# Strided attention in blocks of one residue group instead of blocks of three, and another order for batch 0

## The chip, the cores and the metric

The kernel runs on one core of one Trainium2 chip. A core has a matrix engine (TensorE, PE in the profile, with its weight loads listed as PEld), VectorE (DVE), ScalarE (ACT), GpSimd (POOL) and SyncE (SP). Here POOL and SP also issue the transfers: POOL those that change the type from fp32 to bf16 on the way, SP the plain ones and the transposing ones. The metric is the device time of one execution in microseconds.

## What is computed

Eight batches of eight heads, 576 positions, head size 64. Heads 0 to 3 attend to the last 32 positions ("local"), heads 4 to 7 to all earlier positions with the same residue modulo 32 ("strided"). The outputs of the heads stand side by side as x, with 4608 rows of 512, and go through two matrix products with a squared ReLU between them.

```python
mask_local = (rel >= 0) & (rel < stride)                      # stride = 32
mask_strided = (rel >= 0) & (pos[None, :] % stride == pos[:, None] % stride)
scores = np.where(masks[None, :, :, :], scale * q @ k.T, -1e9)
attn = softmax(scores)
x = (attn @ v).transpose(0, 2, 1, 3).reshape(B * S, H * D)    # 4608 x 512
out = np.maximum(x @ w_in, 0) ** 2 @ w_out                    # 512 -> 2048 -> 512
```

## The kernel before

**Units.** A unit `u` is one pair of heads of one batch, `u = 4 * b + p`; pairs 0 and 1 are local, 2 and 3 strided. A local pair is cut in six blocks of 96 queries, each with 128 keys. A strided pair is cut by residues: positions with equal residue modulo 8 (or 16) form a small dense problem with a mask.

**Strided blocks.** In batches 0 and 1 (`u` up to 7) a strided head has eight blocks, one for each `j = position mod 8`, of 72 positions each. From batch 2 on the kernel before uses the residue modulo 16: 36 positions for each of 16 residues, three residues together in one block of 108 and two in the last of 72, so three blocks for each half of a head (`KB`, `BLK`, lines 39 to 41). `mask_blk` is the mask for them. In the output step the sums come from a column of ones that stands beside V in the tile `vs`.

**Steps of a unit.** `step_T` transposes Q and K of a local pair on PE, `step_TS` those of the strided pairs of batches 0 and 1. `step_S` forms the scores (lines 342 and 350), ACT takes the exponential (360), VectorE multiplies by the mask (367). `step_D` multiplies by V (436) in two parts of six blocks, each into one PSUM bank, and VectorE divides by the sum (446, 447). `step_E` brings the result into `xt`, which holds x transposed: by PE and a copy (483, 485), by a transposing transfer of `x_l` (469), or, for the strided pairs of the last two batches, through DRAM (`x_d`, 463 and 465). `step_N` and `step_O` take the place of D and E for the strided pairs of batches 0 and 1.

**PSUM.** There are eight banks in three rings: `ph` (2), `py` (1) and `pt` (5). Scores take four `pt` banks, each part of D one, each E on PE one.

**Order.** Everything is written out by hand. `first_steps` lists batch 0. Then a list `groups` holds the two products chunk by chunk (512 rows of x each): `mm1` is the first product with ReLU on ACT (511) and the square on VectorE (514), `mm2` the second (545). Before each group the loop takes as many attention steps as `due` says, which spreads each batch's steps over the groups before the first chunk that needs them. Loads hang on group numbers (`second`, `plan`). All engines run their own instructions in that program order.

**Transfers.** POOL issues, in this order for batches 2, 3 and 4: the rows of Q and K of local pairs (135), the copies `q_d`, `k_d` of strided Q and K into DRAM in bf16 (172), then, behind a gate that waits for the transposed `kT_s` (line 626), V of the local pairs (`vl`, 235 and 236) and V of the strided pairs (`vs`, 637). SP transposes `q_d` and `k_d` into `qT_s` and `kT_s` (178), stores the output (553), and for batch 4 first waits in `hold_sync` (630) until the last strided V has landed. For batches 5 to 7 SP loads Q, K (119), V (218 and 251), and POOL casts them (145, 225, 226, 257, 258). In batch 0 POOL loads V of both local pairs with one pair of transfers (235, 236), before w_in (692).

Of the kernel before, what the change touches and what calls it, by code (L numbers as in the profile page):

```python
# [14 lines left out]
def kernel(  # L15
# [23 lines left out]
    PS16 = NA * STRIDE // 16  # L39
    KB = 3 * PS16  # L40
    BLK = ((0, KB), (KB, KB), (2 * KB, S // 2 - 2 * KB))
    V0 = 4
# [36 lines left out]
    mask_blk = singles.tile([KB, 1, S // 2], BF16)  # L79
    vl_all = singles.tile([128, NV, 2, NL, VP], BF16, name="vl")  # L80
    vls = [vl_all[:, i] for i in range(NV)]
    vss = [singles.tile([KB, 2, 3, 2 * D + 8], BF16, name=f"vs{i}") for i in range(NV)]
# [84 lines left out]
    def cast_str_dram(b):  # L167
        for name, src in (("q", q), ("k", k)):
            t = dram.tile([2 * S, 2 * D], BF16, name=f"{name}_d")
            tv = t.rearrange("(h j p) c -> h p j c", h=4, j=8)  # L170
            for h in range(4):
                nc.gpsimd.dma_start(out=tv[h], in_=src[b, 4 + h].rearrange("(p j r) d -> p j (r d)", j=8, r=2))  # L172
            big[b, name] = t

    def transpose_str(b):
        for name in "qk":
            o = strT.tile([128, NJ // 2, 4 * SP_], BF16, name=f"{name}T_s").rearrange("c a n -> c (a n)")
            nc.sync.dma_start_transpose(out=o, in_=big.pop((b, name)))
            came[b] = o[0:1, 0:1]
            for i in range(2):  # L180
                st.setdefault(4 * b + 2 + i, {})[name + "T"] = o[:, S * i:S * (i + 1)]
# [49 lines left out]
    def load_v_local_sw(b):  # L231
        i = (2 * b) % NV
        t = vl_all[:, i:i + 2].rearrange("p u h t d -> p (u h t) d")[:, :, 0:D]
        src = v[b, 0:4].rearrange("h (t p) d -> p (h t) d", p=QL)
        nc.gpsimd.dma_start(out=t[32:128], in_=src)  # L235
        nc.gpsimd.dma_start(out=t[0:32, 1:4 * NL], in_=src[64:96, 0:4 * NL - 1])
        for u in range(2):
            st.setdefault(4 * b + u, {})["v"] = vls[i + u]

    def v_str_pieces(u):  # L240
        b, p = units[u]
        for h in range(2):
            vv = v[b, 2 * p + h].rearrange("(p x r) d -> p x (r d)", x=8, r=2)
            for j in range(3):
                n = 3 if j < 2 else 2
                yield slice(PS16 * j, PS16 * (j + 1)), h, slice(0, n), vv[:, j:j + 3 * n - 2:3, :]

    def load_v_str(u, eng):
        t = v_st.tile([KB, 2, 3, 2 * D], FP32, name="v_st")
        for rows, h, blks, src in v_str_pieces(u):  # L250
            eng.dma_start(out=t[rows, h, blks], in_=src)
        st.setdefault(u, {})["vf"] = t

    def cast_v_str(u):
        s = st[u]
        t = vss[v_slot(u)]
        nc.gpsimd.tensor_copy(t[:, :, 0:2, V0:V0 + 2 * D], s["vf"][:, :, 0:2])
        nc.gpsimd.tensor_copy(t[0:BLK[2][1], :, 2, V0:V0 + 2 * D], s["vf"][0:BLK[2][1], :, 2])
# [56 lines left out]
    def step_S(u, at_once=False):  # L315
# [3 lines left out]
        blocks = not local and u > 7  # L319
        w, n = (QL, NL) if local else (SP_, NJ)  # L320
        kn = 128 if local else KB if blocks else SP_
        hn = 3 if blocks else n // 2
        e = es[u % 4]
        s["e"] = e
        pss = [[None, None], [None, None]]
        for half in range(2):
# [7 lines left out]
            for i in range(hn):  # L334
                t = half * hn + i
                klo = w * t
                for row in range(2):
                    rows = slice(64 * row, 64 * row + 64)
                    if blocks:
                        lo, m = BLK[i]  # L340
                        cols = slice(S // 2 * half + lo, S // 2 * half + lo + m)
                        nc.tensor.matmul(pss[row][half][0:m, lo:lo + m], kT[rows, cols], qT[rows, cols],  # L342
                                         start=True, stop=True)
                        continue
# [7 lines left out]

        for row in range(2):
            for half in range(2):
                unread[id(pss[row][half])] = u

        def expo(row, half):
# [526 lines left out]
```

## Time and profile before

| what | value |
|---|---|
| median of 3 runs | 325.71 us (325.20 to 325.84) |
| profiled execution, its run's time | 325.71 us |
| its span on the core | 324.0 us |
| mean granted TensorE clock | 0.984 |
| PE busy | 303.7 us, 94% |
| VectorE, ScalarE, GpSimd busy | 148.8, 167.5, 112.9 us |
| transferred | 40.76 MB in 113918 packets |

The span is what the profiler saw on the core; the run's time has 1.7 us more around it. Times of a timeline or chain are microseconds from the start of the span. In a list of waits the numbers are the total, how often, and the longest. A group line has the busy time in us, the mean of one instruction in ns, and behind the second bar the time that the engine stood idle just before these instructions, with what ended it. In the rows of tenths each figure is a fortieth of the span, about 8.1 us.

### The profile page before, as it was taken

What the parts mean: (1) busy time and instruction counts of PE and PEld (TensorE: products, weight loads), DVE (VectorE), ACT (ScalarE), POOL (GpSimd) and SP (SyncE); (2) the same over time, 40 slices, a digit from 0 to 9 for tenths busy, and PEclk for the clock granted to TensorE, in tenths of its full rate; (3) what the DMA queues carried; (4) which work ended last, traced back from release to release, by engine and by line L of the source; (5) the groups of instructions that cost most, each with busy time, mean ns of one, the idle gap of its engine ahead of it and who ended that gap; (6) DMA issues with size and microseconds to landing.
All of it is one profiled execution on the core that took longest, in us unless ns stands there. A gap on an engine that the chain in (4) does not pass through costs nothing.

```text
span 324.0 us, 6032 instructions
## 1 busy us (share of the span) xinstructions
PE 303.7 (94%) x2256; PEld 149.6 (46%) x2256; DVE 148.8 (46%) x389; ACT 167.5 (52%) x346; POOL 112.9 (35%) x170
## 2 busy tenths in 40 slices
PE   7999999979699966999899999999999999999995
PEld 3555454545355532444344444444444444444444
DVE  4458645557456760455555666652532222222200
ACT  4768548856548751455455556554344444344411
POOL 8653421891769963591307721500000000000000
PEclk9999999999979996999999999999999999999999
DMA  8999999979999999889975999534131011001021
GB/s 160 174 202 202 191 193 148 171 92 130 175 136 142 86 120 194 189 109 207 201 164 125 202 213 178 128 85 120 46 75 51 33 55 45 32 32 34 32 97 65
DMA packets 113918, 40.76 MB, mean 126 GB/s; under 512 B 96546, under 2 KB 108898, under 8 KB 113890
## 3 DMA queue, kind: packets, MB, share of 16 engines
q0 software_dynamic: 49120, 15.02, 42.5%
q1 hardware_dynamic: 64770, 25.38, 36.0%
q8 instruction: 17, 0.28, 0.4%
q14 instruction: 11, 0.09, 0.1%
HBM read 37.64 MB, written 13.57 MB: 158 GB/s over the span
## 4 chain that ended last, share of the span: by engine, by line
PE 57%; DMA 22%; POOL 12%; issue 5%; SPq 2%; ACT 1%; DVE 1%; POOLq 0%; DVEq 0%
PE py L545 23%; PE ph L505 23%; DMA vl<-in_v_dram 7%; PE ph L545 5%; POOL vs L637 4%; DMA xt<-x_l 3%; DMA kT_s<-k_d 3%; DMA w_in_b<-in_moe_w_in_dram 3%; DMA k_st<-in_k_dram 2%; POOL q_d L172 2%; PE pt L436 2%; POOL k_d L172 1%; DMA x_d<-x_s 1%; POOL vl L235 1%; PE ph L527 1%
## 5 line engine op out<-in xcount | busy, mean ns | idle before, releaser
L505 PE MATMUL ph<-xt,w_in_b 128*128 128x512 bf16 x552 | 141.1, 381 | 2.5 <-DMA xt<-x_l 1.8
L511 ACT ACTIVATE r<-ph 128x512 bf16<-128x512 f32 x138 | 82.3, 597 | 97.8 <-PE ph L505 96.6
L514 DVE TENSOR_TENSOR g_sb<-r 128x512 bf16<-128x512 bf16 x144 | 62.3, 435 | 124.3 <-ACT r L511 123.7
L545 PE MATMUL py<-w_out_b,g_sb 128*128 128x512 bf16 x400 | 104.5, 384 | 0.0
L505 PEld LDWEIGHTS <-w_in_b 128*128 128x128 bf16 x576 | 53.2, 98 | 60.9 <-issue 4.5
L545 PEld LDWEIGHTS <-g_sb 128*128 128x128 bf16 x560 | 51.4, 99 | 58.0 <-issue 4.5
L360 ACT ACTIVATE e<-pt 128x288 bf16<-128x288 f32 (+2 forms) x128 | 45.8, 410 | 15.8 <-PE pt L350 8.1
L545 PE MATMUL ph<-w_out_b,g_sb 128*128 128x512 bf16 x144 | 36.0, 387 | 2.1 <-ACT r L511 2.1
L436 PEld LDWEIGHTS <-e 128*128 128x128 bf16 (+1 forms) x336 | 17.7, 99 | 17.3 <-issue 6.4
L637 POOL DMA_DIRECT2D vs<-in_v_dram x36 | 22.6, 635 | 4.1 <-DMA vl<-in_v_dram 1.6
L549 ACT COPY y<-py 128x512 f32<-128x512 f32 x25 | 14.6, 585 | 7.0 <-PE py L545 6.7
L172 POOL DMA_DIRECT2D k_d<-in_k_dram x24 | 15.7, 658 | 4.6 <-DMA w_out_b<-in_moe_w_out_dram 1.8
L172 POOL DMA_DIRECT2D q_d<-in_q_dram x24 | 15.8, 664 | 2.7 <-DMA w_out_b<-in_moe_w_out_dram 2.2
L447 DVE TENSOR_TENSOR x_l<-pt,rinv 96x384 bf16<-96x384 f32 x28 | 15.5, 553 | 1.0
L446 DVE RECIPROCAL rinv<-pt 96x6 f32<-96x6 f32 (+1 forms) x52 | 9.8, 189 | 12.1 <-PE pt L436 12.0
L225 POOL CAST vl<-vl_st 128x768 bf16<-128x768 f32 x6 | 5.4, 893 | 27.7 <-DMA vl_st<-in_v_dram 15.1
L436 PE MATMUL pt<-vl,e 128*128 128x65 bf16 x168 | 10.5, 199 | 4.1 <-DMA vl<-in_v_dram 4.1
L367 DVE TENSOR_TENSOR e<-e,mask_full 128x576 bf16<-128x576 bf16 x28 | 13.2, 478 | 1.4 <-ACT e L360 1.2
L447 DVE TENSOR_TENSOR x_s<-pt,rinv 108x384 bf16<-108x384 f32 x24 | 13.4, 558 | 0.8
L549 ACT COPY y<-ph 128x512 f32<-128x512 f32 x9 | 5.2, 583 | 13.4 <-PE ph L545 13.4
L342 PE MATMUL pt<-qT_s,kT_s 64*108 64x108 bf16 x144 | 6.3, 220 | 5.6 <-DMA kT_s<-k_d 5.6
L367 DVE TENSOR_TENSOR e<-e,mask_blk 108x576 bf16<-108x576 bf16 x24 | 11.1, 481 | 0.7 <-ACT e L360 0.7
(120 smaller groups left out, 213.1 us busy)
## 6 DMA issues: line engine op xcount, KB each, us to landing
out_dram<-y SPq DMA_DIRECT2D x35, 256.0 KB
w_out_b<-in_moe_w_out_dram POOLq DMA_DIRECT2D x4, 512.0 KB, 15.2
q_d<-in_q_dram POOLq DMA_DIRECT2D x24, 72.0 KB, 5.0
k_d<-in_k_dram POOLq DMA_DIRECT2D x24, 72.0 KB, 5.4
q_st<-in_q_dram SPq DMA_DIRECT2D x12, 144.0 KB
k_st<-in_k_dram SPq DMA_DIRECT2D x12, 144.0 KB
vl_st<-in_v_dram SPq DMA_DIRECT2D x12, 144.0 KB
vl<-in_v_dram POOLq DMA_DIRECT2D x5, 288.0 KB, 6.1
```

The costliest lines, as they stand in the source:

```text
L172: nc.gpsimd.dma_start(out=tv[h], in_=src[b, 4 + h].rearrange("(p j r) d -> p j (r d)", j=8, r=2))
L360: nc.scalar.activation(e[0:kn, lo:lo + S // 2], pss[row][half][0:kn, 0:S // 2], AF.Exp, scale=scale)
L367: nc.vector.tensor_tensor(x, x, m, op=ALU.mult)
L436: nc.tensor.matmul(po[:, n, :], e[0:kn, pos:pos + 128], rhs, start=True, stop=True)
L446: nc.vector.reciprocal(rinv[0:w], po[0:w, :, dc:dc + 1])
L447: nc.vector.tensor_tensor(x, po[0:w, :, x0:x0 + D], rinv[0:w].to_broadcast([w, 6, D]), op=ALU.mult)
L505: nc.tensor.matmul(ph, w_in_b[:, kk, 128 * ff:128 * (ff + 1)], xt[kk][:, 512 * c:512 * (c + 1)], start=(kk == order[0]), stop=(kk == order ...
L511: nc.scalar.activation(r, ph, AF.Relu)
L514: later(1, lambda: nc.vector.tensor_tensor(g[:, ff, :], r, r, op=ALU.mult))
L545: nc.tensor.matmul(py, g[:, ff, 128 * j:128 * (j + 1)], w_out_b[:, ff, :], start=(ff == 0), stop=(ff == 15))
L549: nc.scalar.copy(y, py)
L637: nc.gpsimd.dma_start(out=t[rows, h, blks, V0:V0 + 2 * D], in_=src)
```

## The change

Strided pairs of batches 2 to 7 have eight blocks of 72 per head, as batches 0 and 1 have. `mask_blk`, `KB`, `BLK` and the two-residue layouts go.

- The copies `q_d` and `k_d` become one transfer each for the four heads, 16 rows of 9216 elements, in place of four transfers of 36x8x128. The transposes read 288 rows of 512 in place of 1152 rows of 128.
- V of a strided pair is loaded by one transfer for a head (72x8x64 into `vs`) in place of three; on SP (batches 5 to 7) by one of 72x2x512 for a pair in place of six. `x_d` is written by one transfer in place of six.
- `step_S` forms 16 products of 72 for 12 of 108 or 72; `step_D` has 16 blocks in three parts (6, 6, 4) for 12 in two; `step_E` on PE has eight transposes for six.
- Batch 0: V of each local pair is loaded by its own two transfers; `step_S` of unit 3 takes its exponentials half by half with part 1 of D of unit 0 between the halves; the copies of `x` of units 0 and 1 go to VectorE; pair 1 comes ahead of pair 2 in `first_order`; the late constants are written ahead of the loads of batch 1.

```diff
 def cast_str_dram(b):
     for name, src in (("q", q), ("k", k)):
-        t = dram.tile([2 * S, 2 * D], BF16, name=f"{name}_d")
-        tv = t.rearrange("(h j p) c -> h p j c", h=4, j=8)
-        for h in range(4):
-            nc.gpsimd.dma_start(out=tv[h], in_=src[b, 4 + h].rearrange("(p j r) d -> p j (r d)", j=8, r=2))
+        t = dram.tile([4 * SP_, NJ * D], BF16, name=f"{name}_d")
+        nc.gpsimd.dma_start(
+            out=t.rearrange("(x y) c -> x (y c)", x=16),
+            in_=src[b, H // 2:H].rearrange("h (x y) d -> (h x) (y d)", x=4))
...
-def load_v_local_sw(b):
-    i = (2 * b) % NV
+def load_v_local_sw(b, u0=0, nu=2):
+    i = (2 * b + u0) % NV
...
 def load_v_str(u, eng):
-    t = v_st.tile([KB, 2, 3, 2 * D], FP32, name="v_st")
-    for rows, h, blks, src in v_str_pieces(u):
-        eng.dma_start(out=t[rows, h, blks], in_=src)
+    b, p = units[u]
+    t = v_st.tile([SP_, 2, NJ * D], FP32, name="v_st")
+    eng.dma_start(out=t, in_=v[b, 2 * p:2 * p + 2].rearrange("h (p j) d -> p h (j d)", j=NJ))
...
 def step_S(u, at_once=False, between=None):
...
-                if blocks:
-                    lo, m = BLK[i]
-                    cols = slice(S // 2 * half + lo, S // 2 * half + lo + m)
-                    nc.tensor.matmul(pss[row][half][0:m, lo:lo + m], kT[rows, cols], qT[rows, cols], ...)
-                    continue
...
+        if between:
+            for row in range(2):
+                expo(row, half)
+            between(half)
...
 def step_D(u, part):
+    if is_local(u):
+        w, kn, n0, n1, tot = QL, 128, 6 * part, 6 * part + 6, 2 * NL
+    else:
+        w, kn, tot = SP_, SP_, NBS
+        n0, n1 = ((0, 6), (6, 12), (12, 16))[part]
...
 def step_E(u):
-        for j in range(3):
-            for r in range(2):
-                nc.sync.dma_start(out=xv[:, 2 * j + r:2 * j + r + 6 * m - 5:6, :], in_=x[PS16 * j:PS16 * (j + 1), r, 0:m])
+        nc.sync.dma_start(out=xd.rearrange("(p j) c -> p (j c)", j=NJ), in_=x.rearrange("p n d -> p (n d)"))
...
-    copy = nc.scalar.copy if u < 12 else nc.vector.tensor_copy
+    copy = nc.scalar.copy if 1 < u < 12 else nc.vector.tensor_copy
...
-first_order = (0, 2, 1, 3)
+first_order = (0, 1, 2, 3)
...
-  (ts("k", 0, v_), 0), (ts("k", 1, s_), 1), (S_(2), 0), (D_(0, 0), 0), (D_(0, 1), 0), (S_(3), 0),
-  (D_(1, 0), 0), (n(2), 1), (E_(0), 0), (n(3), 0), (D_(1, 1), 0),
-  (o(2), 0), (lambda: part((a,)), 0), (E_(1), 0), (o(3), 0), (lambda: part((b,)), 0),
-  (lambda: part((c,)), 0), (lambda: part((d,)), 0)]
+  (ts("k", 0, v_), 0), (ts("k", 1, s_), 1), (S_(2), 0),
+  (D_(0, 0), 0), (lambda: step_S(3, between=lambda half: None if half else step_D(0, 1)), 0), (n(2), 1),
+  (D_(1, 0), 0), (E_(0), 1), (D_(1, 1), 0), (n(3), 0), (lambda: part((a,)), 0), (E_(1), 0),
+  (o(2), 0), (lambda: part((b,)), 0), (lambda: part((c,)), 0), (o(3), 0), (lambda: part((d,)), 0)]
...
 def load_v_str_direct(b):
     for u in (4 * b + 2, 4 * b + 3):
         t = vss[v_slot(u)]
-        for rows, h, blks, src in v_str_pieces(u):
-            nc.gpsimd.dma_start(out=t[rows, h, blks, V0:V0 + 2 * D], in_=src)
+        h = 2 * units[u][1]
+        for i in range(2):
+            nc.gpsimd.dma_start(out=t[:, NJ * i:NJ * (i + 1), 0:D],
+                                in_=v[b, h + i].rearrange("(p j) d -> p j d", j=NJ))
...
-load_v_local_sw(0)
+load_v_local_sw(0, 0, 1)
+load_v_local_sw(0, 1, 1)
...
-loads_1()
 late_constants()
+loads_1()
```

## The prediction

> **What bounds the kernel now.** I read the page's head first, then the waits of PE, then PE's timeline around each wait, then the timelines of POOL, SP and ACT back from there. The first fence is the page: PE is busy 94% of the span, and its clock falls to 7 and 6 tenths in two slices near 90 and 124 us.
>
> ```profile
> PE 303.7 (94%) x2256; PEld 149.6 (46%) x2256; DVE 148.8 (46%) x389; ACT 167.5 (52%) x346; POOL 112.9 (35%) x170
> PE   7999999979699966999899999999999999999995
> PEclk9999999999979996999999999999999999999999
> ```
>
> So the end is set by PE, and only two things can move it: matmuls that PE has more or fewer of, and the holes. From 18 us on the holes sum to 14.0 us. The next fence, the waits of PE (total, times, longest), names them.
>
> ```profile
> PE pt L342 <- DMA kT_s<-k_d: 5.6, 1, 5.6
> PE pt L436 <- DMA vl<-in_v_dram: 4.1, 3, 3.0
> PE ph L545 <- ACT r L511: 2.1, 1, 2.1
> PE ph L505 <- DMA xt<-x_l: 1.8, 2, 1.6
> ```
>
> In PE's timeline three lie between 70 and 125 us: 2.13 us before 73.41, 3.04 + 0.70 us before 90.08, and 5.55 us before 124.39. The two longer ones cost twice: a group of four 128x512 matmuls that else takes 0.865 us took 1.69 us at 90.80 and 1.68 to 1.71 us from 125.09 to 130.72, under a granted clock of 0.50. Counted against the same instructions at full rate, 90.08 to 92.84 lost 1.3 us, and 124.39 to 130.72 lost 3.1 us (6.33 us for work of 3.19). Stalls and clock in this stretch: 2.13 + 3.74 + 5.55 + 1.3 + 3.1 = 15.8 us.
>
> The third fence follows them back. Columns: start, duration, engine, line, operation, and in brackets the idle time before.
>
> ```profile
> 56.88 0.37 POOL L626 COPY vl<-kT_s 1x1 bf16<-1x1 bf16 x1 [6.31 <-DMA kT_s<-k_d]
> 59.48 3.78 POOL L637 DMA_DIRECT2D vs<-in_v_dram  x6
> 63.89 3.73 POOL L637 DMA_DIRECT2D vs<-in_v_dram  x6 [0.63 <-DMA vl<-in_v_dram]
> 68.97 2.65 POOL L172 DMA_DIRECT2D q_d<-in_q_dram  x4
> 71.61 1.95 POOL L172 DMA_DIRECT2D k_d<-in_k_dram  x3
> 72.04 0.83 ACT L145 COPY q_l<-q_st 96x768 bf16<-96x768 bf16 x1 [2.55 <-DMA q_st<-in_q_dram]
> 77.80 1.22 SPq L178 DMA_TRANSPOSE kT_s<-k_d  x1
> 82.37 0.18 POOL L626 COPY vl<-kT_s 1x1 bf16<-1x1 bf16 x1 [7.96 <-DMA kT_s<-k_d]
> 90.08 0.43 PE L436 MATMUL pt<-vl,e 128*128 128x65 bf16 x5 [0.70 <-DMA vl<-in_v_dram]
> ...
> 114.69 0.30 SPq L630 DMA_DIRECT2D hold<-vs  x1
> 116.84 2.06 SPq L178 DMA_TRANSPOSE kT_s<-k_d  x1
> 124.39 0.76 PE L342 MATMUL pt<-qT_s,kT_s 64*108 64x108 bf16 x12 [5.55 <-DMA kT_s<-k_d]
> ```
>
> To be seen: all three holes hang on POOL's queue of DMA issues. After the gate at 56.88 POOL spends 8.1 us on twelve pieces of V (batch 2), issues batch 3's q/k rows at 67.6, and needs until 74.4 for eight copies q_d/k_d (batch 3). ACT's cast waits for the late rows until 72.04; that is PE's first hole. The transposes on SP wait for the copies, kT_s starts at 77.80 and lands at 82.35; only then does the gate let V of batch 3 go (82.9), which lands at 90.08: the second hole. The same string, one batch on, puts the last V piece of batch 4 so late that the hold on SP passes at 114.69, kT_s starts at 116.84 and PE waits until 124.39. A second rule shows at 89.3 to 93.7: successive V pieces wait for vl, vl, q_st and k_st, the transfers eight issues earlier. So POOL has at most eight transfers out, and many small ones use them up.
>
> The prices are in the groups (busy us, mean ns of one):
>
> ```profile
> L637 POOL DMA_DIRECT2D vs<-in_v_dram x36 | 22.6, 635 | 4.1 <-DMA vl<-in_v_dram 1.6
> L172 POOL DMA_DIRECT2D q_d<-in_q_dram x24 | 15.8, 664 | 2.7 <-DMA w_out_b<-in_moe_w_out_dram 2.2
> L172 POOL DMA_DIRECT2D k_d<-in_k_dram x24 | 15.7, 658 | 4.6 <-DMA w_out_b<-in_moe_w_out_dram 1.8
> L235 POOL DMA_DIRECT2D vl<-in_v_dram x5 | 6.0, 1195 | 1.1 <-POOL vl L626 0.7 <-DMA w_in_b<-in_moe_w_in_dram 0.5
> ```
>
> **The change, part by part.**
>
> *POOL, batches 2 to 4.* V goes from twelve issues per batch to four of 72x8x64, q_d and k_d from eight to two. An issue grows slowly with its pieces: 0.635 us at 108 (36x3x128), 0.66 at 288, 0.70 at 384 (q_st), 0.77 at 736 (L236), 1.20 at 2304 (L235). Four at 576 pieces: 0.74 us each by interpolation, 3.0 us against 7.6. Two copies at 0.66 make 1.3 against 5.25. POOL is 8.5 us shorter per batch, before waits.
>
> *First hole.* From the same gate at 56.88: vl to 59.45, four V issues to 62.4, the rows to 63.8, both copies to 65.1 (the one eight back, vl, has landed at 63.6). The rows thus go out at 62.4 and not 67.6; with the 4.4 us that they took they land near 66.8, ACT wants them at 69.5. Gain 2.13 us; next late is nothing before 84 us. That q_d and k_d of batch 2 also go out up to 10 us sooner (five waits of 0.53 to 2.15 us at 39 to 49 us fall away) I count at nothing, since w_out lies ahead of them in the queue until 47.2 us.
>
> *Second hole.* Copies are out at 65.1 and not 74.4. With the old 3.4 us to kT_s and 4.55 us to its landing the gate opens at 73.1, not 82.4; vl goes at 73.6 and lands 7.2 us later, 80.8. PE now comes for it at 86.14 - 2.13 = 84.0. Margin 3.2 us; gain 3.74 + 1.3 = 5.0 us. With the margin used up each us costs one.
>
> *Third hole.* POOL goes on from 73.6: vl, rows and V to 79.4, copies behind the landing at 80.8 to 82.1, two memsets 1.4, vl of batch 4 to 85.5, V of batch 4 (its buffers were read last by PE near 84) to 88.5, landed near 92. SP reaches the hold about 94 (before: its store and transpose up to 101.8, less 7.2 us), so the hold waits for nothing. kT_s lands, at the 7.5 us that it took, by 104; PE comes for it at 118.84 - 7.2 = 111.7. Gain 5.55 + 3.1 = 8.7 us.
>
> *SP later.* The hold had set SP back by 12.8 us, and its queue still shows it: 1.61 us of PE wait for xt<-x_l at 158.27, 0.15 at 190.20, 0.39 for xt<-x_d at 223.15. In the new kernel SP starts those loads earlier, v_st falls from twelve issues (5.83 us at 132.09) to two, and x_d from six (2.62 us at 209.13) to one. Bounds: nothing gained, or all 2.15. I take 1.9, since SP's backlog is what ends the wait. Nearest prices of the wide v_st and x_d rows are L123's issues, 0.39 and 0.44 us.
>
> *PE.* Each of the 12 strided pairs has 16 output matmuls for 12. Six take 0.19 us in a row (76.95 to 77.14), so four more are 0.127 us, 1.5 us in all, straight onto the end. Scores: 16 of 72 columns took 0.41 us (45.27 to 45.68), 12 of up to 108 took 0.41 (69.65 to 70.06): nothing. Back transposes: eight of 72 for six of up to 108; sixteen 72-column matmuls took 0.38 us at 50.21, so eight fit in the 0.27 us that the six took: nothing.
>
> *VectorE.* A third reciprocal (0.19 us) and 6 + 6 + 4 blocks for 6 + 6 of 108 partitions: about 0.57 us more per pair, estimated from 0.558 us for six blocks; 6.8 us in all. It lies beside PE: from 60 to 70 us VectorE was 66% busy and PE never stopped. The third part takes one more of the five pt banks, which PE could have to wait for. No row shows that; bounds 0 and 3.4 us (half of the added work uncovered), I take 0.4, since the pt waits shown, but for those on transfers, are 0.2 us.
>
> *The start.* Pair 1 of V as a load of its own adds two issues, about 1.2 us (1.20 + 0.81 become about 3.2), ahead of w_in. The third w_in piece landed at 18.98 for a use at 20.95; the pieces ahead of it landed before POOL's issues at 16.41 and 18.06, used at 18.05 and 19.86. D of pair 0 loses its 0.17 us wait, the x copies leave ACT (12.7 of 20 us busy) at 0.63 us each, the first product no longer stands behind O(2) (0.45 us). Against it vl of batch 1 waits for a w_in piece as before and PE had 0.40 us of wait for it at 37.75. Bounds -0.8 and +1.5; I take 0: what is won before 38 us ends in that wait.
>
> *Transfers.* Transposes have the same bytes in another shape (288 rows of 512 for 1152 of 128): the same as L178, between 3.06 and 7.5 us. The new copy has 16 rows of 9216 elements. No row shows such long ones; the nearest are the pieces it replaces, 5.0 and 5.4 us to landing, and q_st's 12 us in a full queue; I take 5.
>
> V's runs go from 256 B to 128 B and from 1152 to 2304 per batch. In this trace 3040 runs of 128 B (vl at 57.55) landed in 6.06 us, so 2304 are 4.6 us at most, beside 3.1 us for one old piece; V of batch 4, issued by 88.5, lands by 92 or 93. Here a page speaks against the change: the Trainium skill, "DMA: Bandwidth & Descriptors", section Specifications, puts the least transfer for full rate at 512 B and says that below it the engine reads, modifies and writes. By that rule alone V would be dearer than now, the margin of the third hole smaller, and the sum the same as long as it lasts.
>
> **Sum**, against the profiled execution's span of 324.0 us: -2.1 - 5.0 - 8.7 - 1.9 + 1.5 + 0.4 = -15.8, span 308.2. The run of that profile took 325.71 us, 1.7 over its span, and 325.71 is also the median. So 309.9, rounded to 310.
>
> **Rivals.**
> *Half is kept.* The moved transfers meet the w_out loads and the stores, the margins of 3.2 and 7.7 us are eaten, and half of the second and third hole stays: gain 2.1 + 6.9 less 1.9 = 7, 318.6 us. For it: DMA shares of 1.0 to 1.5 in this stretch. Against: 72 to 83 GB/s at 60 to 70 and 110 to 120 us, 198 at 20 to 38.
> *DMA was the limit all along.* Only the first hole closes, PE's extra work takes it back: -2.1 + 1.9, 325.5. Against: POOL's issues stand end to end in the chain, and V pieces land 3.1 us after issue, without a backlog.
> *Slower.* The long copy gives each engine one row of 36 KB. Issued at 65.1, it has until 77.8 to be no later than now: 12.7 us. If it takes 16, the second and third holes each grow by 3.3 us: 6.6 - 2.1 + 1.9 = 6.4, 332 us. Against: the pieces' 5 us, and 590 KB over 16 engines at the 198 GB/s shown is 3 us.
>
> **How the numbers follow.** Likeliest 0.68: its own range is 308 (start -0.8, bank -0.4, SP -0.25, the 0.40 us wait at 37.75) to 316 (+1.5, +3.0, +1.9). Half kept 0.20, DMA limit 0.06, slower 0.06. About 0.2%, 0.65 us, can be told from no change; of the DMA-limit case half is inside it. Faster 0.90, same 0.03, slower 0.07. The range 307.5 to 319 takes in 0.6 us of spread between runs below, the half-kept case above, and leaves out the two last.
>
> **What would show it.** PE's waits: no wait over 1 us for kT_s, vl or ACT r between 60 and 130 us, the clock at 9 in these slices. POOL: four V issues near 0.74 us, two copies near 0.66. The hold passes without waiting. PE has 113 more matmuls and 1.5 us more work. The prediction is wrong if q_d takes over 12 us to land, if PE waits for VectorE on pt banks by more than 3 us, or if a new hole opens behind 130 us because PE now comes 15 us sooner for batches 5 to 7.

## The result, and the profile after

The changed kernel takes 310.19 us (median of 4 runs, 310.03 to 311.04). The kernel before, run beside it, took 325.77 us (4 runs, 325.20 to 329.90). The ratio is 0.9501, with a 95% interval from 0.9422 to 0.9581. The forecast was 310.0 us, with a range from 307.5 to 319. A few runs below lie over 1.5% above the fastest of their kernel (some of the kernel before, one of reorder, one of start_new2); medians and ranges include them (without its one, reorder's median is 321.97 us and start_new2's 327.52), ratios don't.

The profiled execution of the changed kernel took 311.04 us, 0.85 over the median, with a span of 309.3 us and a mean granted clock of 1.0. Read it in the same order as before: first the head of the page.

```profile
PE 301.0 (97%) x2369; PEld 150.0 (49%) x2369; DVE 159.3 (51%) x407; ACT 166.1 (54%) x344; POOL 75.5 (24%) x105
PE   8998999999999999999999999999999999999995
PEclk9999999999999999999999999999999999999999
```

PE is busy 97% of the span where it was 94%, and the clock stands at 9 in every slice: the 7 and the 6 near 90 and 124 us are gone. PE has 113 matmul records more (2369 for 2256), yet less busy time, as none behind the start runs at half clock now. POOL fell from 112.9 to 75.5 us. The second view is PE's waits.

```profile
PE py L546 <- DVE xt L648: 1.3, 1, 1.3
PE ph L487 <- DVE xt L405: 1.2, 1, 1.2
PE pt L427 <- DVE e L358: 0.3, 1, 0.3
```

The list had 13.6 us of waits for kT_s, vl, ACT's r and xt; now not one of its lines names a transfer. The first one, 1.3 us, stands ahead of PE's first instructions, as it did before; the second, 1.2 us for VectorE's `xt` (line 405), lies in the start too, at 24.51 us. From there on PE's timeline shows two holes only, 0.20 and 0.31 us.

The third view is the string of events from POOL's queue to PE, in the timelines of POOL, SP and PE. Columns are start, duration, engine, line and operation, and in brackets the idle time before.

```profile
56.67 0.18 POOL L610 COPY vl<-kT_s 1x1 bf16<-1x1 bf16 x1 [18.37 <-DMA kT_s<-k_d]
59.20 3.24 POOL L622 DMA_DIRECT2D vs<-in_v_dram  x4
62.43 0.72 POOL L130 DMA_DIRECT2D q_st<-in_q_dram  x1
63.79 0.57 POOL L165 DMA_DIRECT2D q_d<-in_q_dram  x1
64.32 0.56 POOL L165 DMA_DIRECT2D k_d<-in_k_dram  x1
71.58 1.30 SPq L173 DMA_TRANSPOSE qT_s<-q_d  x1
72.99 1.29 SPq L173 DMA_TRANSPOSE kT_s<-k_d  x1
76.54 0.18 POOL L610 COPY vl<-kT_s 1x1 bf16<-1x1 bf16 x1 [11.66 <-DMA kT_s<-k_d]
85.05 0.54 POOL L165 DMA_DIRECT2D k_d<-in_k_dram  x1 [0.89 <-DMA vl<-in_v_dram]
86.28 0.35 PE L427 MATMUL pt<-vl,e 128*128 128x65 bf16 x6
...
103.02 0.30 SPq L614 DMA_DIRECT2D hold<-vs  x1
105.71 1.30 SPq L173 DMA_TRANSPOSE kT_s<-k_d  x1
```

The gate of batch 2 (56.67) is where it was (56.88). V of batch 2 now takes 3.24 us of POOL in place of 8.1 with its wait, so batch 3's rows go out at 62.43 and not 67.6, and its copies are out at 64.88 and not 74.4. But then 6.7 us pass until SP's transpose of `q_d` starts at 71.58, so the gate of batch 3 opens at 76.54: 5.8 us sooner than before, not the 9.5 us by which POOL is ahead. POOL's `k_d` at 85.05 waits for the transfer eight places ahead, the second and smaller piece of `vl` (line 238); the large one is a place ahead of that. So `vl` has landed then, and PE comes for it at 86.28, 1.2 us later. That is all the slack there is.

The groups give the prices of one issue (busy us, mean ns of one, idle before):

```profile
L622 POOL DMA_DIRECT2D vs<-in_v_dram x12 | 9.7, 818 | 0.1
L165 POOL DMA_DIRECT2D q_d<-in_q_dram x6 | 3.2, 526 | 0.0
```

### The profile page after: what moved, and what is told of

It reads as the page before. It is cut to its first block, busy times and chain, and to the rows that moved or that the text cites. A ratio compares the mean times of both kernels' runs of the same rounds, so it can differ in the third digit from the quotient of the medians.

```text
span 309.3 us, 6118 instructions
## 1 busy us (share of the span) xinstructions
PE 301.0 (97%) x2369; PEld 150.0 (49%) x2369; DVE 159.3 (51%) x407; ACT 166.1 (54%) x344; POOL 75.5 (24%) x105
## 4 chain that ended last, share of the span: by engine, by line
PE 91%; DVE 4%; ACT 2%; DMA 1%; issue 0%; DVEq 0%
PE ph L487 38%; PE py L527 28%; PE ph L527 9%; PE pt L344 4%; PE pt L427 3%; PE pt L487 1%; PE pt L288 1%; DVE x_l L440 1%; PE pt L527 1%; PE ph L509 1%; DMA q_st<-in_q_dram 1%; PE pt L463 1%; DVE g_sb L496 1%; DVE e L358 1%; PE py L546 0%; PE pt L332 0%
## 5 line engine op out<-in xcount | busy, mean ns | idle before, releaser
L496 DVE TENSOR_TENSOR g_sb<-r 128x512 bf16<-128x512 bf16 x144 | 65.2, 454 | 104.8 <-ACT r L493 103.5
L323 ACT ACTIVATE e<-pt 72x288 bf16<-72x288 f32 (+1 forms) x128 | 45.7, 407 | 9.5 <-PE pt L344 9.3
L427 PEld LDWEIGHTS <-e 128*128 128x128 bf16 (+1 forms) x384 | 20.4, 97 | 14.6 <-DVE e L358 0.7
L440 DVE TENSOR_TENSOR x_s<-pt,rinv 72x384 bf16<-72x384 f32 (+1 forms) x36 | 18.3, 509 | 1.2
L358 DVE TENSOR_TENSOR e<-e,mask_str 72x576 bf16<-72x576 bf16 x28 | 13.5, 493 | 3.8 <-ACT e L323 3.7
L439 DVE RECIPROCAL rinv<-pt 96x6 f32<-96x6 f32 (+2 forms) x64 | 11.8, 184 | 6.2 <-PE pt L427 5.9
L358 DVE TENSOR_TENSOR e<-e,mask_full 128x576 bf16<-128x576 bf16 x28 | 13.6, 485 | 1.9 <-ACT e L323 1.7
L427 PE MATMUL pt<-vs,e 72*128 72x65 bf16 x192 | 12.1, 194 | 0.7 <-DVE e L358 0.3
L140 POOL CAST q_l<-q_st 96x768 bf16<-96x768 f32 x6 | 5.4, 908 | 21.4 <-DMA q_st<-in_q_dram 21.3
L622 POOL DMA_DIRECT2D vs<-in_v_dram x12 | 9.7, 818 | 0.1
L344 PEld LDWEIGHTS <-kT_s 64*72 64x72 bf16 x256 | 6.0, 113 | 7.0 <-issue 6.2
```

The lines of the kernel that those rows point to most:

```text
L323: nc.scalar.activation(e[0:kn, lo:lo + S // 2], pss[row][half][0:kn, 0:S // 2], AF.Exp, scale=scale)
L344: nc.tensor.matmul(pss[row][half][0:kn, w * i:w * (i + 1)], lhsT, rhs, start=u > 3, stop=True, skip_group_check=u < 4)
L358: nc.vector.tensor_tensor(x, x, m, op=ALU.mult)
L427: nc.tensor.matmul(po[:, n - n0, :], e[0:kn, pos(n):pos(n) + 128], rhs[0:kn, src(n), 0:D + 1], start=True, stop=True)
L439: nc.vector.reciprocal(rinv[0:w, 0:m], po[0:w, 0:m, D:D + 1])
L440: nc.vector.tensor_tensor(x, po[0:w, 0:m, 0:D], rinv[0:w, 0:m].to_broadcast([w, m, D]), op=ALU.mult)
```

## The experiments

The theory to be tested is that of the prediction, A: the number of transfers that POOL issues for V and the copies set the three holes. Rivals are B, that the other order of batch 0 brings the gain or a part of it; C, that the form of the data (block of 72, other runs and rows in the transfers) does; and D, that `hold_sync` makes the third hole by itself. The kernel before was run beside each set: it took 325.39 us (11 runs) on the chip of start_old, start_new, o3_early and no_hold, and 327.28 (7 runs) and 326.70 (13 runs) on that of the others. Each ratio is to the kernel before on the same chip.

### 1. Which half of the diff: the blocks or batch 0

start_old is the changed kernel with the kernel before's batch 0: what is left of the change is the blocks of 72 and their transfers.

```diff
-first_order = (0, 1, 2, 3)
+first_order = (0, 2, 1, 3)
...
-copy = nc.scalar.copy if 1 < u < 12 else nc.vector.tensor_copy
+copy = nc.scalar.copy if u < 12 else nc.vector.tensor_copy
...
-load_v_local_sw(0, 0, 1)
-load_v_local_sw(0, 1, 1)
+load_v_local_sw(0)
...
-late_constants()
 loads_1()
+late_constants()
```

The list of steps in `first_steps` is the kernel before's as well.

> The changed kernel with batch 0 as it was before: V of both local pairs in one pair of loads, O(2) and O(3) ahead of the first product's later parts, x copies of units 0 and 1 on ScalarE, pair 2 ahead of pair 1, loads of batch 1 ahead of the late constants. Theory A (the whole gain comes from POOL's shorter queue from batch 2 on; the new batch 0 costs time): the start is shorter by the 1.2 us wait before 24.51 and its refill, and one warm matmul, together 1.6 us: 308.6 us, or up to 0.6 more if V of batch 3, which landed only 1.2 us ahead of PE, is late now. Theory B (the new batch 0 has a part in the gain): slower than the changed kernel, above 310.8.

Measured: 308.72 us (6 runs, 308.07 to 311.27), ratio 0.9494 (0.9459 to 0.9528). The blocks and their transfers give all of the gain, and by the medians 1.5 us more than the whole change; B falls as a cause of the gain.

start_new is the mirror image, the kernel before with the changed kernel's batch 0.

```diff
-first_order = (0, 2, 1, 3)
+first_order = (0, 1, 2, 3)
...
-copy = nc.scalar.copy if u < 12 else nc.vector.tensor_copy
+copy = nc.scalar.copy if 1 < u < 12 else nc.vector.tensor_copy
...
-load_v_local_sw(0)
+load_v_local_sw(0, 0, 1)
+load_v_local_sw(0, 1, 1)
...
+late_constants()
 loads_1()
-late_constants()
```

The list of steps, and `step_S` with exponentials between its halves, are the changed kernel's as well.

> The kernel before with the changed batch 0 alone. Theory A: PE comes up to 1.6 us later to the first hole, which POOL's queue ends and not PE, so the hole at 71 us shrinks by as much: 325.2 to 326.5 us. Theory B: faster than before by 1 us or more, below 324.7.

Measured: 333.59 us (4 runs, 333.40 to 333.81), ratio 1.0246 (1.0215 to 1.0276). That is a miss: it is 8 us slower, where at most 1 was expected. POOL's timeline of this run shows why, and the list of PE's waits what follows:

```profile
28.77 0.48 POOL L720 TENSOR_SCALAR_AFFINE_SELECT mask_blk<-mask_blk 108x108 bf16<-108x108 bf16 x1 [15.03 <-DVE mask_blk L718]
29.33 0.69 POOL L135 DMA_DIRECT2D q_st<-in_q_dram  x1
```

```profile
PE pt L294 <- DVE q_l L145: 2.8, 1, 2.8
```

In the kernel before, `late_constants` ends with an `affine_select` on POOL for `mask_blk`. Written ahead of `loads_1` it stands in POOL's queue ahead of batch 1's rows and waits 15.03 us for VectorE; the rows go out at 29.33 us, and PE waits 2.8 us for their cast. In the changed kernel `late_constants` has no POOL instruction, so the same two swapped lines put nothing ahead of the rows there, and these go out at 13.01 us. start_new2, shown against start_new, puts those two lines back and keeps the rest of the new batch 0:

```diff
-late_constants()
 loads_1()
+late_constants()
```

> The kernel before with the changed kernel's batch 0, as start_new, but with late_constants written behind loads_1 as the kernel before has it. My theory of start_new's 333.6 us: there the affine_select on mask_blk, which the changed kernel doesn't have, stood ahead of batch 1's loads in POOL's queue and waited 15.03 us for VectorE. If that is the whole of it, this run gives 325.2 to 327 us (the order of batch 0 alone is worth 0 to +1.5 us as the changed kernel's start showed, +2.5 in the profiled execution with 0.86 of it the clock). Rival: batch 0's order itself costs the kernel before more than it costs the changed one, because its later waits have no slack to take a late start: 328 to 333 us. The issue of q_st of batch 1 on POOL should go out at about 14 us instead of 29.33 by the first and the 2.83 us wait for q_l at 34 be gone.

Measured: 327.68 us (10 runs, 324.38 to 331.18) beside 326.70 for the kernel before (13 runs, 324.31 to 329.44), ratio 1.0020 (0.9979 to 1.0061). POOL's timeline has the rows at their old place, and the constant's instruction behind them:

```profile
13.82 0.69 POOL L135 DMA_DIRECT2D q_st<-in_q_dram  x1
32.72 0.29 POOL L720 TENSOR_SCALAR_AFFINE_SELECT mask_blk<-mask_blk 108x108 bf16<-108x108 bf16 x1
```

So the swap was the whole of the 8 us, but for at most 2 us that this run's interval can't exclude (0.6% of some 326 us). A line order that is harmless in one kernel was expensive in the other, because of one instruction in the function that was moved.

### 2. The number of POOL's issues, with blocks and bytes kept

v12 is the changed kernel with V cut into three transfers per head by partitions; the runs, the bytes and the blocks of 72 are unchanged, but POOL issues twelve per batch again, as the kernel before did.

```diff
-nc.gpsimd.dma_start(out=t[:, NJ * i:NJ * (i + 1), 0:D],
-                    in_=v[b, h + i].rearrange("(p j) d -> p j d", j=NJ))
+vv = v[b, h + i].rearrange("(p j) d -> p j d", j=NJ)
+for c in range(3):
+    p3 = slice(24 * c, 24 * c + 24)
+    nc.gpsimd.dma_start(out=t[p3, NJ * i:NJ * (i + 1), 0:D], in_=vv[p3])
```

> The changed kernel with strided V of batches 2 to 4 issued in twelve pieces of 24x8x64 per batch, same bytes, runs and blocks. Theory A (number and time of POOL's issues): 12 times about 0.67 us for 3.25, 4.8 us more per batch: the gate of batch 3 at 81.3 and not 76.5, its V lands 3.5 us after PE's 86.3, the hold of batch 4 passes some 10 us later than 103: holes of 3.5 and 3 to 5 us plus the clock, about 320 us. Theory C (the size of blocks, runs and packets makes the difference, not the issues): 310 us, unchanged.

Measured: 316.44 us (4 runs, 316.15 to 316.79), ratio 0.9673 (0.9614 to 0.9732). The first copy on POOL, the gate, the hold on SP and the holes of PE:

```profile
68.44 0.56 POOL L165 DMA_DIRECT2D q_d<-in_q_dram  x1
81.07 0.18 POOL L610 COPY vl<-kT_s 1x1 bf16<-1x1 bf16 x1 [11.56 <-DMA kT_s<-k_d]
87.06 0.19 PE L427 MATMUL pt<-vl,e 128*128 128x65 bf16 x1 [0.38 <-DMA vl<-in_v_dram]
109.97 0.30 SPq L614 DMA_DIRECT2D hold<-vs  x1
117.80 0.47 PE L344 MATMUL pt<-qT_s,kT_s 64*72 64x72 bf16 x16 [2.04 <-DMA kT_s<-k_d]
```

POOL comes to `q_d` 4.65 us later (68.44 for 63.79), the gate of batch 3 falls back by 4.5 us, from 76.54 to 81.07, and the second and third hole are there again at 0.73 (two waits, 0.38 and 0.35) and 2.04 us. All waits behind the start are 3.6 us more than in the changed kernel, and behind 117.80 PE takes 5.71 us for work of 4.05. It is less than the 320 us that was expected, as both holes are smaller than the 3.5 and 3 to 5 us expected. The edit makes eight more issues per batch and, with them, smaller transfers; these landed sooner (3.5 us in the median for 8.2), so it is not a longer landing that makes the holes.

c8 cuts each copy in four by columns, eight copies per batch as before, and leaves V alone:

```diff
-nc.gpsimd.dma_start(
-    out=t.rearrange("(x y) c -> x (y c)", x=16),
-    in_=src[b, H // 2:H].rearrange("h (x y) d -> (h x) (y d)", x=4))
+to = t.rearrange("(x y) c -> x (y c)", x=16)
+fr = src[b, H // 2:H].rearrange("h (x y) d -> (h x) (y d)", x=4)
+for i in range(4):
+    cs = slice(2304 * i, 2304 * i + 2304)
+    nc.gpsimd.dma_start(out=to[:, cs], in_=fr[:, cs])
```

> The changed kernel with each copy q_d and k_d of batches 2 to 7 cut in four issues of 16x2304, same bytes. Theory A: 3.3 us more of POOL per batch: V of batch 3 lands 2 us after PE comes for it, plus a clock loss of about 1 us, the third hole stays shut: about 313 us. Theory C: 310 us, or faster, since shorter rows land sooner.

Measured: 310.28 us (4 runs, 310.04 to 310.81), ratio 0.9486 (0.9428 to 0.9545): a miss, it costs nothing.

```profile
64.08 2.04 POOL L169 DMA_DIRECT2D q_d<-in_q_dram  x4
70.08 0.49 POOL L169 DMA_DIRECT2D k_d<-in_k_dram  x1 [0.97 <-DMA k_st<-in_k_dram]
71.78 1.33 SPq L175 DMA_TRANSPOSE qT_s<-q_d  x1
77.03 0.18 POOL L612 COPY vl<-kT_s 1x1 bf16<-1x1 bf16 x1 [6.47 <-DMA kT_s<-k_d]
```

The last copy leaves POOL at 70.57 and not 64.88, 5.7 us later, but SP's first transpose starts at 71.78 (changed kernel 71.58) and the gate opens at 77.03 (76.54). `q_d` has 5.7 us from the end of its last issue to the transpose, and `k_d` 2.8 us (70.57 to 73.33), where the long ones had 7.2 and 8.1: the cut copies go out later and land at the same time. POOL's time for them is hidden there. v12c8 has both edits together:

> The changed kernel with both cuts: POOL has as many issues for batches 2 to 4 as in the kernel before, PE and VectorE have the changed blocks. Theory A: the holes of before come back, 322 to 328 us. Theory C: within 1 us of the changed kernel's 310.

Measured: 321.32 us (4 runs, 320.96 to 321.73), ratio 0.9822 (0.9762 to 0.9883), just below the 322 to 328 that was expected.

```profile
PE pt L346 <- DMA kT_s<-k_d: 4.7, 1, 4.7
PE pt L429 <- DMA vl<-in_v_dram: 1.7, 1, 1.7
PE ph L529 <- ACT r L495: 1.5, 1, 1.5
```

All three holes are back in their old order of size: 4.7 us for kT_s (5.6 in the kernel before), 1.7 for vl (4.1), 1.5 for ACT's r (2.1). With the same blocks and the same bytes, on one chip, 12 issues for V and the copies of a batch (c8) take 310.28 us, 14 (v12) 316.44 and 20 (v12c8) 321.32; the changed kernel has 6, the kernel before 20. So A holds for 11.0 us. The whole is 15.6 by the result and 17.0 by the kernel before on this chip (327.28), so two thirds or more are shown, and C falls as the main cause. (`cast_str_dram` also serves batches 5 to 7, so there too c8 and v12c8 issue eight copies for two.) It isn't a price for each issue, though: six more for the copies alone cost nothing, eight more for V alone 6.2 us, and the copies on top of them 4.9.

What remains is that v12c8's span is 320.0 us and the kernel before's 324.0. Their holes account for most of it: 0.6 us less before ACT's r, 3.4 less for vl (1.68 without a slower clock for 3.74 + 1.3), 0.9 less for kT_s, 2.15 less for xt and the 0.40 us before 37.75 make 7.4 less; 1.4 of work on PE, 1.8 in the start (23.82 for 22.03) and a wait of 0.7 for VectorE make 3.9 more, together 3.5 of the 4.0. The cut copies of v12c8 issue in 0.51 us where the kernel before's take 0.66, which would make the holes smaller. This sum is worked out, and no run tests it by itself; how much of the rest is the form of the data stays open.

### 3. The same pieces in another order

reorder is the kernel before with batch 3's rows and copies written ahead of V of batch 2; nothing is made shorter.

```diff
-second(29, lambda: load_v_local_gated(2), lambda: load_v_str_direct(2), rows(3), lambda: cast_str_dram(3))
+second(29, lambda: load_v_local_gated(2), rows(3), lambda: cast_str_dram(3), lambda: load_v_str_direct(2))
```

> The kernel before with one line changed: on POOL's queue the rows and copies of batch 3 go ahead of strided V of batch 2; every issue and every block stays. Theory A (what counts is when POOL gets to an issue): rows out at 59.5 and not 67.6, the first hole goes; the gate of batch 3 opens near 74.5 and not 82.4, the second hole goes; the third shrinks from 5.6 to about 2.5 us: about 313.5 us, up to 2 us more if V of batch 2 is late at 75. Theory C: 324 to 326.

Measured: 322.04 us (4 runs, 319.39 to 325.43), ratio 0.9804 (0.9701 to 0.9908), where 313.5 was expected.

```profile
75.82 0.31 PE L436 MATMUL pt<-vs,e 108*128 108x65 bf16 x5 [1.22 <-DMA vs<-in_v_dram]
76.01 0.18 POOL L626 COPY vl<-kT_s 1x1 bf16<-1x1 bf16 x1
110.18 0.30 SPq L630 DMA_DIRECT2D hold<-vs  x1
119.18 0.76 PE L342 MATMUL pt<-qT_s,kT_s 64*108 64x108 bf16 x12 [6.97 <-DMA kT_s<-k_d]
```

The gate opens at 76.01 us, like the changed kernel's, and the first two holes are gone but for a new one of 1.22 us, V of batch 2 itself. But the third hole grew from 5.55 to 6.97 us: PE comes 6.6 us sooner there (112.21 for 118.84), and POOL still has as many issues to do before V of batch 4 lets the hold pass at 110.18 (114.69 before). An order that closes a hole gave the time to the next one here; of these runs, only those with the shorter queue close all three.

no_hold is the kernel before without the wait on SP, for rival D:

```diff
-second(64, lambda: hold_sync(4))
```

> The kernel before without the hold of SP before the transposes of batch 4. Theory A says that POOL's queue makes all three holes; the third goes through the hold. Copies of batch 4 were issued until 102.1 and land near 107, so without the hold the transposes start near 107 and end near 114, before PE's 118.8: the third hole and its clock loss go, 8.7 us, about 317 us. A rival within it: the hold only hides that the transposes compete with V's loads, and they then end no sooner: 324 to 326 us.

Measured: 321.80 us (4 runs, 320.33 to 323.52), ratio 0.9888 (0.9841 to 0.9936), where 317 was expected.

```profile
117.97 2.61 POOL L172 DMA_DIRECT2D k_d<-in_k_dram  x4
120.55 1.34 SPq L178 DMA_TRANSPOSE qT_s<-q_d  x1
128.50 5.47 SPq L251 DMA_DIRECT2D v_st<-in_v_dram  x12
138.04 0.63 PE L350 MATMUL pt<-qT,kTl 64*128 64x96 bf16 x12 [3.98 <-DMA kTl<-k_l]
```

The 5.55 us for kT_s at 124 us are gone, and 3.98 us for `kTl` of batch 5 at 138 us are new. SP's transposes of batch 5 now wait for copies that POOL issues until 120.58; behind them stand twelve issues of V on SP (5.47 us), and only then come the transposes of `k_l`. So the hold made the hole's place, and only a part of its cost: without it the kernel is 1.1% faster (0.6 to 1.6%), some 3.6 us, where 8.7 were expected. D falls as the whole cause; the rest stands one step further back, in the same queue of POOL and in SP's behind it.

### 4. Smaller terms

o3_early writes the last output step of batch 0 one place sooner in the changed kernel, so that VectorE has time for it.

```diff
-(lambda: part((c,)), 0), (o(3), 0), (lambda: part((d,)), 0)]
+(o(3), 0), (lambda: part((c,)), 0), (lambda: part((d,)), 0)]
```

> The changed kernel with O(3) moved ahead of the third part of the first product. Theory A: the wait of 1.2 us for VectorE before the fourth part goes, 309.0 us. If the hole would move to another place of the start, 310.2.

Measured: 309.64 us (5 runs, 309.29 to 309.75), ratio 0.9508 (0.9483 to 0.9533). The 1.2 us wait is gone. Shown are the changed kernel's fourth part of the first product, and the same part in o3_early:

```profile
24.51 0.59 PE L487 MATMUL ph<-xt,w_in_b 128*128 128x512 bf16 x2 [1.23 <-DVE xt L405]
```

```profile
23.07 0.59 PE L487 MATMUL ph<-xt,w_in_b 128*128 128x512 bf16 x2
```

The part starts 1.4 us sooner; 0.35 of it comes from ahead of the product's second part (20.22 for 20.57). The medians differ by 0.55 us, half of the 1.2 that was expected; where the rest goes is not shown.

sp12 cuts SP's loads `v_st` and stores `x_d` of the changed kernel into six each for a pair, as many as before.

```diff
-eng.dma_start(out=t, in_=v[b, 2 * p:2 * p + 2].rearrange("h (p j) d -> p h (j d)", j=NJ))
+vv = v[b, 2 * p:2 * p + 2].rearrange("h (p j) d -> p h (j d)", j=NJ)
+for h in range(2):
+    for c in range(3):
+        cs = slice(D * NJ * c // 3 // 4 * 4, D * NJ * (c + 1) // 3 // 4 * 4)
+        eng.dma_start(out=t[:, h, cs], in_=vv[:, h, cs])
...
-nc.sync.dma_start(out=xd.rearrange("(p j) c -> p (j c)", j=NJ), in_=x.rearrange("p n d -> p (n d)"))
+xv, xn = xd.rearrange("(p j) c -> p (j c)", j=NJ), x.rearrange("p n d -> p (n d)")
+for c in range(6):
+    cs = slice(2 * D * NJ * c // 6, 2 * D * NJ * (c + 1) // 6)
+    nc.sync.dma_start(out=xv[:, cs], in_=xn[:, cs])
```

> The changed kernel, but on SP's queue the load v_st of a strided pair is cut into 6 DMAs and the store x_d of a pair into 6, as many as the kernel before issues; the bytes are the same. It sets a price on the term 'SP later' (1.9 us of waits for xt in the kernel before). If SP's number of issues made those waits, some of them come back: 311 to 312 us, with PE waits for xt behind 150 us. If they came from SP being held until late (hold_sync there 9 us later, the transposes behind it), nothing comes back: 310.0 to 310.5 us and no wait of PE behind 150 us.

Measured: 311.75 us (4 runs, 310.67 to 312.60), ratio 0.9565 (0.9519 to 0.9610). No wait of PE for xt comes back, although the time lies 1.2 to 1.6 us over the other runs of the changed kernel; what of it is the edit is not settled, as the profiled run itself took 310.67. In v12c8 the other half was missing: there the hold passes at 113.08, nearly as late as before, with wide loads on SP, and no wait for xt either. The kernels that have both, narrow loads and a late hold, show them: the kernel before (2.15 us) and reorder (2.6 for x_l, 0.6 for x_d). no_hold has narrow loads and no hold, and 1.1 us of them (0.56 and 0.55) remain; there the copies keep SP until 120.55. So in these runs SP's backlog reaches PE where loads are narrow and SP is kept until late, by the hold or otherwise.

copies_first writes rows and copies of batch 3 ahead of V of batch 2 in the changed kernel, as reorder does in the kernel before.

> The changed kernel with rows(3) and the two copies of batch 3 (q_d, k_d) written ahead of V of batch 2 in POOL's queue, so that they go out 4 x 0.82 = 3.3 us sooner. In the changed kernel q_d is out at 63.8 us and landed at 71.58, 7.8 us later, where I had taken 5. If the landing is a fixed time behind the issue, q_d lands near 68.3 us and kT_s and the gate of batch 3 come 3.3 us sooner (gate near 73.2). If it is set by the bytes queued ahead of it (V of batch 2 is taken from ahead of it too), it lands sooner still, near 67 to 68, with 6 to 7 us from issue to landing. If something that does not move with POOL's order sets it (the transfers of vl and the rows), it stays at 70 to 71.6. The time stays at 309.7 to 310.6 us in all cases, as PE waits for no transfer in the changed kernel.

Measured: 310.50 us (one run). The copies, the transposes that wait for them, and the gate:

```profile
60.90 0.55 POOL L165 DMA_DIRECT2D q_d<-in_q_dram  x1
61.91 3.29 POOL L622 DMA_DIRECT2D vs<-in_v_dram  x4
68.65 1.80 SPq L173 DMA_TRANSPOSE qT_s<-q_d  x1
71.73 1.62 SPq L173 DMA_TRANSPOSE kT_s<-k_d  x1
75.45 0.29 POOL L610 COPY vl<-kT_s 1x1 bf16<-1x1 bf16 x1 [10.26 <-DMA kT_s<-k_d]
```

`q_d` goes out 2.9 us sooner and its transpose starts 2.9 us sooner: 7.7 us from issue to landing in both. V ahead of it or behind it makes no difference to `q_d` in this run. But `k_d`, with V right behind it, now takes 10.3 us where it took 8.0, and the gate opens 1.1 us sooner and not 3.3. To be first in POOL's queue is worth only a part of what the queue shows; how V lengthens the landing of a copy ahead of it, this run does not show.

best is start_old with V of batch 0's local pairs loaded pair by pair, the one piece of the new batch 0 that could help by itself.

> The changed kernel with the kernel before's order of batch 0 (pair 2 ahead of pair 1, halves of strided scores not split by outputs, x copies of pairs 0 and 1 on ScalarE, loads_1 ahead of late_constants), but V of local pairs of batch 0 loaded pair by pair as the changed kernel does. Beside start_old (308.72 us), whose only other difference is that V of batch 0 comes in one piece: there PE waited 0.3 us for vl in the start. If the pair-by-pair load is worth that wait, 308.3 to 308.6 us; if its two further POOL issues (near 0.7 us each) push the loads of weights behind them, whose last one PE waited 0.7 us for, 308.7 to 309.8 us.

Measured: 308.71 us (4 runs, 308.29 to 309.30), ratio 0.9475 (0.9434 to 0.9515). Its median is start_old's 308.72: the 0.3 us wait for vl in the start is gone and brings nothing that the runs can tell. Both medians are 1.5 us, 0.5%, below the changed kernel's (310.19, and 310.28 and 310.50 of its variants c8 and copies_first). The ratios to the kernel before don't separate them, as the spread of that kernel's runs is in the intervals.

## Why the prediction was right, and where it wasn't

The sum was 324.0 - 15.8 = 308.2 us of span; the profile has 309.3. The time was forecast as 310.0 and measured as 310.19. Step by step:

| step of the prediction | predicted, us | measured, us |
|---|---|---|
| first hole | -2.13 | gone |
| second hole | -5.0, margin 3.2 | gone, margin 1.2 |
| third hole | -8.7, margin 7.7 | gone, margin 1.1 to 4.0 (estimate, see landing times) |
| SP later | -1.9 | all three waits gone, -2.15 |
| four more output matmuls for 12 pairs | +1.5 | +1.4 (what the sum below leaves) |
| VectorE and the pt banks | +0.4 | +0.5 (two waits, 0.20 for a bank and 0.31 for `e`) |
| the start | 0 (-0.8 to +1.5) | +2.5 in the profile, 1.6 without PE's slower first matmuls |

*The holes.* Their mechanism was right: the runs with more issues bring them back, one by one. Behind the start, from the fourth part of the first product (22.03 and 24.51 us) to the last group (317.01 and 302.18), the changed kernel is 17.3 us shorter. The holes of before in that stretch are 14.0 us of waits and 4.4 of clock, and seven times 0.17 us: groups of matmuls else overlap by that much in the timeline (one of 0.59 us at 21.67, the next at 22.10), and a wait takes this away as well. That makes 19.6. In the changed kernel 0.51 and two times 0.17 are left, 0.85. 19.6 - 0.85 - 17.3 leaves 1.4 us for the added matmuls. In the timeline a third part of four takes 0.12 us (106.09 to 106.21), which for 12 pairs is the same.

*The start* is the term that was mis-sized. I set it to 0 and argued that gains before 38 us would end in the 0.40 us wait for vl there. That wait is gone, and the first product's fourth part comes 2.5 us later. 0.86 us of it are PE's first matmuls, which were slower in that execution: two of 512 columns at 5.55 us took 1.05 us for 0.60, and the group of line 288 that started at 7.90 us before starts at 8.76. The clock that the profile lists is 1.00 there in both, so the cause is open; c8's profile has 0.72 us less of it. Of the other 1.6 us, 1.4 come from O(3), which in the new order stands directly ahead of that part: PE waits 1.23 us for the VectorE copy (line 405), and loses the overlap of 0.17. The last 0.2 are not assigned. best has its first scores at the same 7.22 us as c8 and the old order behind them; the fourth part starts at 21.85 us there and at 23.81 in c8, so inside the changed kernel the new order costs 2.0 us at this place. The diff showed that order, and I counted what left the path there (O(2)) but not what came onto it. By the medians start_old puts the whole of the new batch 0 at 1.5 us, the upper bound that I gave.

*Why the total fits nonetheless.* Two errors of opposite sign: the start cost more (+2.5 in the profile), and the holes and matmuls gave more than I counted (-1.4: the seven overlaps 1.2, the wait at 37.75 0.4, SP 0.25, less 0.45 that the changed kernel still has). 308.2 + 2.5 - 1.4 = 309.3. The profiled run is 0.85 over the median, about what the slower first matmuls cost. The mechanism was right; that the total came within 0.2 us is luck.

*Landing times* were wrong, and only the margins paid for it. I took 5 us for the long copies from the pieces they replace; they took 7.7 and 8.0 in batch 3, and 8.3 to 13.8 in the others that I followed (2, 4 and 5). I said that 2304 runs of V would land in 4.6 us at most; V's pieces of batches 2 to 4 took 4.5 to 12.0. POOL's V issue was 0.82 us and not 0.74, the copy's 0.53 and not 0.66. The gate of batch 3 opened at 76.54 and not 73.1, and the hold, for which I had no wait, waited 7.4 us and passed at 103.02 and not 94. kT_s of batch 4 went out at 105.71; with the 4.55 to 7.5 us that it took before it lands at 110.3 to 113.2, and PE, 2.5 us later than I had it, takes it at 114.31 without a wait. v12 shows how near that was: eight more issues per batch, and 2.04 us of it are a hole. best shows the same for the second hole: PE comes for `vl` at 83.81, its second piece, issued at 77.37, lands 6.2 us later, and 0.2 us are left. That the margins I had sized wrongly still held is luck too.

*The rivals.* "Half is kept" had the right mechanism, the margins were eaten by transfers in the same queue; but 1.2 us of the second and an estimated 1.1 to 4.0 of the third were left. "DMA was the limit all along" is out with the transfers that PE no longer waits for, although the copies landed later than I had thought. "Slower" needed 12.7 us for the long copy and 16 to reach its price; it takes 7.7 in batch 3, and the copy cut in four ends at the same time (71.78 for 71.58).

*The page that spoke against it.* The Trainium skill, "DMA: Bandwidth & Descriptors", section Specifications, puts the least transfer for full rate at 512 B. V's pieces with runs of 128 B landed in 8.2 us in the median (4.5 to 12.0) where those of 256 B had 3.3 (2.0 to 7.5), though each new one holds 2.7 to 4 times the bytes. v12 separates the two: its pieces have runs of 128 B and a third of the bytes (24.6 KB, where the old ones had 27.6 or 18.4), and they landed in 3.5 us in the median (2.2 to 7.7). So the longer landing goes with the larger transfer, and the shorter runs cost nothing that shows. Both lengths lie under 512 B, so no run here tests that limit itself. The price fell on the margin, not on the time.

## What to carry to other kernels

When an issuing queue orders many small transfers, count the issues between an event and the transfer that somebody waits for: here 14 issues fewer in each of three batches, and six fewer in the next three, were worth 11 us of some 16, though no byte less was moved. The holes that were closed by order alone (reorder), or by taking one wait away (no_hold), reappeared in part at the next consumer of the same queue; what closed them all was work taken out of the queue. And before moving a function in the program order, look for the one instruction in it that waits: `late_constants` cost some 7 us in one kernel, and in the other it holds no instruction for POOL.

## What the runs showed of the hardware

*A clock that falls after 2 us, or doesn't.* The long waits cost PE half its clock behind them: from 124 to 128 us the kernel before's mean granted clock is 0.50. The stretch from 116 to 132 us in the kernel before and in the changed kernel (columns: busy time of each engine with its instructions, then the clock, the DMA share and GB/s):

```profile
116.00:132.00 16.00, 10.45 (x56) 4.61 (x55) 4.85 (x13) 4.19 (x10) 5.80 (x8) 0.79 1.36 186
```

```profile
116.00:132.00 16.00, 16.00 (x123) 7.76 (x122) 10.70 (x23) 8.84 (x19) 7.30 (x9) 1.00 1.05 195
```

A wait of 2.04 us in v12 (at 117.80) was enough: the clock is 0.81 and 0.76 in the slices from 116 to 120 and from 120 to 124 us. So was one of 2.21 us in start_new2 (at 160.00), with 0.50 in the 2 us behind it. A wait of 2.14 us in reorder (at 154.04) left it at 1.00, as did the kernel before's 2.13 us at 73.41.

```profile
116.00:120.00 4.00, 2.21 (x27) 1.22 (x28) 0.43 (x1) 1.09 (x3) 0.39 (x1) 0.81 1.04 229
120.00:124.00 4.00, 4.00 (x19) 1.66 (x17) 2.20 (x4) 1.47 (x4) 2.14 (x3) 0.76 0.83 181
```

```profile
154.00:158.00 4.00, 3.96 (x34) 1.94 (x34) 0.66 (x2) 1.88 (x5) 0.47 (x1) 1.00 1.03 242
```

The Trainium skill, "TensorE: Matmul & The Clock Gate", Part 1, has a window of some 3.4 us that runs freely, and the clock halved after an idle window. That two waits of nearly the same length fall on either side agrees with a free window; that 2.04 us were enough does not fit the page's 3.4, and here the measurement decides. The two falls in the kernel before cost 1.3 and 3.1 us on top of their waits.

*A full queue hides issue time.* In c8 six more issues, the last one 5.7 us later, moved SP's transpose by 0.2 us; between v12 and v12c8 the same six more cost 4.9 us. The price of an issue doesn't tell which. Neither does the time from a copy's last issue to its transpose: `k_d` has 2.8 us in c8, where the issues are hidden, and 3.4 in the kernel before (74.41 to 77.80).
